# Sliding-window attention block: one V load a tile and sums turned on TensorE for the first four tiles, with a new instruction order

## The chip, the cores and the metric

The kernel runs on one core of a Trainium2 chip. The metric is device time in microseconds (us) of one execution. A core has a matrix engine (TensorE, PE in the profile), a vector engine (VectorE, DVE), an activation engine (ScalarE, ACT), a general engine (GpSimd, POOL), and a sync engine (SP) that here only issues transfers; sixteen DMA engines move the data. Each engine runs its own list of instructions in order and waits on semaphores for the others. Engines work from SBUF, the on-chip memory of 128 partitions; TensorE writes to PSUM, eight banks of 512 fp32 per partition, from which VectorE or ScalarE evict.

## The reference

One transformer block with adaptive layer norm, 2048 tokens, width 512, batch 1, bf16:

```
mod = (silu(c) @ w_mod)          # six vectors of 512: sa, ca, ga, sb, cb, gb
h = layernorm(x) * (1 + ca) + sa
q, k, v = h @ wqkv               # 32 heads of 16
# each token attends to W = 8 keys: itself and 2, 4, ... 14 tokens back (dil = 2)
idx = pos[:, None] - 2 * arange(8);  logits = (q . k[idx]) / 4, masked where idx < 0
o = softmax(logits) @ v[idx]
x = x + ga * (o @ wo)
h = layernorm(x) * (1 + cb) + sb
x = x + gb * ((silu(h @ w1) * (h @ w3)) @ w2)      # inner width 1792
```

## The kernel before

The tokens lie in 16 tiles of 128. Tile T goes through these steps; the line numbers are those of the profile.

- Layer norm statistics on VectorE (L594, L595) with the reciprocal root on GpSimd (L599, L601); the normalized tile is turned by TensorE or by a DMA transpose, and ScalarE applies the modulation (L676, L653). This is done in four groups of four tiles.
- Projections on TensorE: q and k with channels on the partitions (L777, evicted by ScalarE in L785 and L786), v with tokens on the partitions (L796). ScalarE evicts v (L806) into one of six buffers `sb_v`, with the channels put in the order (channel in head, head), and Sync stores it to a scratch tensor in HBM, `v_scratch_dram`. A V buffer is free when its store has landed.
- Logits: VectorE multiplies q by the eight shifted views of k (L827, 4096 products a partition); TensorE sums the products over each head's 16 channels with an indicator `sb_E` (L836), in four column groups of 32 tokens that run side by side. In each group the 32 tokens stand in the order even tokens first, then odd ones: the columns are read at a step of 2. For tile 0 one extra matmul (L833) adds a large negative number where a key lies before the first token; its constant is `sb_before`. Maximum, exponential (ScalarE, L866), sum and division follow for two tiles at a time (L848 to L881).
- The weights of a pair of tiles are turned by TensorE (L891) and evicted by ScalarE into `sb_al` (L895), so that a partition holds one (token pair, window place) combination.
- V load: for each quarter q of the tile one transfer of 128 pieces of 2 KB (L904): partition (t, w) gets the two neighbouring rows of V of token pair t shifted by window place w. Four loads of 256 KB a tile fill the 8 rows a partition of a `sb_vsh` buffer. There are two such buffers, and a third, `sb_vshx`, in the memory of `wqkv` once the projections are over.
- VectorE multiplies V by the weights in place (L911, 4096 elements a partition), and TensorE sums over the window places with the indicator `sb_ind` (L920). ScalarE evicts the sums to `sb_oa` (L926), a DMA transpose turns them into `sb_ot`, and TensorE projects them with `wo` (L944). VectorE adds the result to x (L948).
- The second norm (L616 to L631, GpSimd L626 and L627), and the feed-forward part in six groups of two or four tiles: gate and up on TensorE (L960), SiLU and copy on ScalarE (L966, L970), their product on VectorE (L971, L974), the down projection (L1003, L991), the last addition on VectorE (L1019) and the store of the output from one of four buffers `sb_o`.

The weights are loaded by Sync in pieces; w1 and w3 have four pieces each (`w1_0` to `w3_3`), as has w2. All of Sync's transfers share one queue.

Nothing orders this at run time. `Program.op` records every step with its engine and what it reads and writes. Two literal lists at the end of the file, `ORDER` and `SLOTS`, say in which order the recorded steps stand in the engines' lists, and which buffer each value gets; `place` applies them, `synchronize` derives the waits from them, and `emit` writes the instructions. All transfers are recorded by one helper, so that every one of them has line 124.

Of the kernel before, what the change touches and what calls it, by code (L numbers as in the profile page):

```python
# [266 lines left out]
PACKET = {T: 95 if T < 2 else 122 for T in range(16)}  # L267
WMOD = 66
WARMS = (8, 1, 1, 1, 3)
NVB = 6  # L270
# [4 lines left out]
AVCOL = frozenset(range(16))  # L275
UPACT = frozenset((g, f) for g in range(4) for f in range(14))
GBLATE = False
# [3 lines left out]
def _build(p, A_x, A_wqkv, A_wo, B_w1, B_w3, B_w2, c, w_mod, out):  # L281
# [20 lines left out]
    vshb = [sb([P, 8, D], bf, f"vsh{i}") for i in range(2)]  # L302
# [14 lines left out]
    before = sb([P, W, 2, 16], bf, "before")  # L317
# [28 lines left out]
    osb = [nc.alloc_sbuf_tensor_at(f"sb_o{i}", [P, D], bf, offset=nc.lookup_mloc(wqkv).addr + 8192 + 1024 * i) for i in range(NOB)]  # L346
    vsh_x = nc.alloc_sbuf_tensor_at("sb_vshx", [P, 8, D], bf, offset=nc.lookup_mloc(wqkv).addr)
# [31 lines left out]
    qkv_hold = held(vshpool, [vsh_x]) + held(opool, osb)  # L379

    vc, vident, vcst, vE, vind, vbefore = (Val(n) for n in ("const", "ident", "cst", "E", "ind", "before"))
# [19 lines left out]
    for edge, mult in ((0, 1), (W - 1, -1)):  # L401
# [3 lines left out]
    p.op("pool", lambda e: e.memset(before[:], 0.0), 250, k, w=[vbefore])  # L405
    p.op("pool", lambda e: e.affine_select(out=before[:], in_=before[:], compare_op=ALU.is_ge, fill=BEFORE, base=0,
                                           pattern=[[-DIL, W], [1, 2], [2, 16]], channel_multiplier=0), 400, k, w=[vbefore])
# [10 lines left out]

    def split_rows(a, row):
        return bass.AP(a.tensor, a.offset + row * D, [[D, 2], [2 * D, P // 2], [1, D]])  # L420
# [125 lines left out]
    def gate(i):  # L546
# [24 lines left out]
        p.op("act", lambda e: e.activation(dst[:], bank(vgb), ACT.Copy), c_act(512), k, r=[vgb], w=[vg[i]])  # L571
# [244 lines left out]
    def logits(Ts):  # L816

        vl = Val("ps_l", psum)
        for i, T in enumerate(Ts):
# [10 lines left out]
            def red(e, i=i, T=T, vp=vp):  # L830
                c0 = vl.at * 512 + i * W * 32
                if T == 0:
                    e.matmul(PALL[0:32, c0:c0 + W * 32], ones[:, 0:32], before[:], start=True, stop=False, tile_position=(0, 0))  # L833
                for ft in range(KT):
                    for q in range(4):
                        ins = e.matmul(PALL[32 * q:32 * q + 32, c0:c0 + W * 32], E_sb[:, ft, :], bass.AP(vp.at, ft * P + 32 * q, [[W * KT * P, P], [KT * P, W], [1, 2], [2, 16]]),  # L836
                                       start=(ft == 0 and (T > 0 or q > 0)), stop=(ft == KT - 1), tile_position=(0, 32 * q))
                return ins

            p.op("pe", red, C_RED + (110 if T == 0 else 0), ("lg", T), r=[vp, vE] + ([vbefore, vc] if T == 0 else []), part=[vl], tiled=True)  # L840
# [32 lines left out]
    def softmax(Ts, vl, ve, vx_):  # L873
# [12 lines left out]
        def turn(e):  # L886
            b = bank(vt).bitcast(bf)
            for i in range(n):
                at = b[:, i * 256:(i + 1) * 256].rearrange("p (q y h) -> p q y h", q=4, y=2)
                for y in range(2):  # L890
                    ins = e.transpose(at[:, :, y, :], bass.AP(ve.at[0], i * W * 32 + y * 16 * W, [[2 * W * 32, P], [1, P]]), ident[:])  # L891
            return ins
# [6 lines left out]
    def values(T, i, val):  # L899

        vv = Val("vsh", vshpool)
        loads = []
        for q in range(4):
            p.dma(lambda q=q: vv.at[:, 2 * q:2 * q + 2, :],  # L904
                  bass.AP(v_dram, (PAD + T * P + 32 * q) * D, [[2 * D, 16], [-DIL * D, W], [1, 2 * D]]), ("vl", T), (128, 2048),
                  r=[vv_dram[T]] + ([vv_dram[T - 1]] if T else [vvpad]), part=[vv], group=loads, cost=640, again=PACKET[T])

        def av(e):
            a_w = bass.AP(val.at, i * 8 * H, [[2 * 8 * H, P], [H, 8], [0, DH], [1, H]])
            v_w = bass.AP(vv.at, 0, [[8 * D, P], [D, 8], [H, DH], [1, H]])  # L910
            return e.tensor_tensor(v_w, v_w, a_w, ALU.mult)  # L911

        avs[T] = p.op("dve", av, C_PQ, ("av", T), r=[val], w=[vv], lock=True)
        vo, vt = Val("ps_o", psum), Val("ot", otpool)
        if T in AVCOL:
            def acc(e):
                b = bank(vo)
                for r in range(2):
# [245 lines left out]
```

## Time and profile before

| | |
|---|---|
| median of three runs | 244.95 us (243.38 to 245.19) |
| profiled execution: time, span | 245.03 us, 243.0 us |
| TensorE busy | 232.6 us, 96% of the span |
| VectorE, ScalarE, GpSimd busy | 169.1, 158.3, 23.0 us |
| moved by DMA | 38.33 MB |
| granted TensorE clock | 1.00 |

The span runs from the first to the last instruction of the profiled execution; what its time has beyond the span lies ahead of it and behind. In rows that group instructions stand line, engine, operation, what is written and read, the count, the busy time in us, the mean length of one in ns, and behind the second bar the idle time of the engine just before them, with what ended it. Rows in order of time begin with the start and the length in us. [...] In the page's second part a digit is the busy share of one fortieth of the span, in tenths.

### The profile page before, as it was taken

The numbers are of one execution on the slowest core, as the hardware profiler recorded it, in microseconds if no ns is written. First come the engines' busy times: TensorE is split into PE (matmuls) and PEld (weight loads), VectorE is DVE, ScalarE is ACT, GpSimd is POOL, SyncE is SP. The second block draws the span as 40 slices with busy tenths as digits, with TensorE's granted clock in tenths as the row PEclk, the third lists the DMA queues.
The fourth block names the chain that finished last, engine by engine and source line by source line (L and its number), as shares of the span: only waits on it lengthen the run. The fifth ranks groups of instructions, "written<-read, shape, count | busy, mean of one in ns | idle before, by whom it ended". The sixth has DMA issues, their size and how long they took to land.

```text
span 243.0 us, 4593 instructions
## 1 busy us (share of the span) xinstructions
PE 232.6 (96%) x1789; PEld 134.1 (55%) x1814; DVE 169.1 (70%) x295; ACT 158.3 (65%) x324; POOL 23.0 (9%) x54
## 2 busy tenths in 40 slices
PE   7899999999789999999999999999999999999995
PEld 1665454545357885654444444444655447576874
DVE  5489999999697999999999698366133213155242
ACT  4358597799788978777967798876653674321300
POOL 6421330011001100011000040110000100000000
DMA  5999899599589999699897824884020030011002
GB/s 167 288 361 265 272 298 215 134 272 275 175 196 291 256 242 245 154 214 137 251 227 195 237 65 68 194 182 99 3 65 1 3 86 0 0 46 43 3 23 65
DMA packets 44685, 38.33 MB, mean 158 GB/s; under 512 B 19560, under 2 KB 35960, under 8 KB 44664
## 3 DMA queue, kind: packets, MB, share of 16 engines
q1 hardware_dynamic: 44656, 38.04, 62.6%
q8 instruction: 14, 0.23, 0.4%
q14 instruction: 7, 0.06, 0.1%
q10 hardware_dynamic: 8, 0.00, 0.0%
HBM read 29.62 MB, written 4.21 MB: 139 GB/s over the span
## 4 chain that ended last, share of the span: by engine, by line
PE 65%; DMA 14%; SPq 7%; ACT 6%; DVE 5%; issue 2%; POOL 1%; ACTq 0%
PE pall L960 33%; PE pall L1003 14%; SPq L124 7%; PE pall L777 5%; DMA sb_wm_g<-in_w_mod_dram 4%; DMA sb_ot<-sb_oa 4%; PE pall L944 3%; DMA v_scratch_dram<-sb_v 3%; PE pall L991 3%; PE pall L796 2%; PE pall L920 2%; DMA sb_h<-sb_xn 2%; PE pall L836 2%; ACT sb_h L653 2%; ACT sb_xn L620 1%
## 5 line engine op out<-in xcount | busy, mean ns | idle before, releaser
L960 PE MATMUL pall<-sb_h,sb_w 128*128 128x256 bf16 (+1 forms) x668 | 103.0, 308 | 1.4 <-DMA sb_w<-in_B_w_dram 0.7
L960 PEld LDWEIGHTS pall<-sb_h,sb_w 128*128 128x128 bf16 x672 | 64.4, 98 | 38.0 <-ACT sb_hh L970 1.5
L966 ACT ACTIVATE sb_sg<-pall 128x256 bf16<-128x256 f32 (+1 forms) x84 | 35.0, 453 | 33.5 <-PE pall L960 25.9
L1003 PE MATMUL pall<-sb_w,sb_hh 128*128 128x512 bf16 x187 | 43.2, 379 | 0.6
L827 DVE TENSOR_TENSOR sb_pq<-sb_q,sb_kT 128x4096 bf16<-128x4096 bf16 x16 | 36.3, 2277 | 0.0
L970 ACT ACTIVATE sb_hh<-pall 128x256 bf16<-128x256 f32 (+1 forms) x56 | 26.5, 494 | 10.3 <-PE pall L960 10.3
L1003 PEld LDWEIGHTS pall<-sb_w,sb_hh 128*128 128x128 bf16 x196 | 18.9, 98 | 21.3 <-DVE sb_hh L971 0.6
L974 DVE TENSOR_TENSOR sb_hh<-sb_sg,pall 128x256 bf16<-128x256 bf16 x28 | 11.1, 418 | 26.6 <-PE pall L960 23.3
L911 DVE TENSOR_TENSOR sb_vsh<-sb_vsh,sb_al 128x4096 bf16<-128x4096 bf16 x12 | 27.4, 2286 | 2.4 <-ACT sb_al L895 1.3
L777 PE MATMUL pall<-sb_h,sb_wqkv 128*128 128x512 bf16 x107 | 25.8, 379 | 1.2 <-ACT sb_v L806 0.9
L971 DVE TENSOR_TENSOR sb_hh<-sb_sg,sb_hh 128x256 bf16<-128x256 bf16 (+1 forms) x56 | 17.9, 349 | 7.3 <-ACT sb_sg L966 4.0
L1019 DVE TENSOR_TENSOR sb_o<-pall,sb_x 128x512 bf16<-128x512 f32 (+1 forms) x18 | 11.0, 627 | 13.4 <-PE pall L1003 7.3
L626 POOL TENSOR_SCALAR sb_rs<-sb_var 128x2 f32<-128x2 f32 x8 | 4.9, 608 | 145.5 <-ACT sb_xn L620 145.5
L777 PEld LDWEIGHTS pall<-sb_h,sb_wqkv 128*128 128x128 bf16 x112 | 10.3, 98 | 12.0 <-ACT sb_v L806 1.4
L944 PE MATMUL pall<-sb_wo,sb_ot 128*128 128x512 bf16 x60 | 15.7, 379 | 0.9 <-DMA sb_ot<-sb_oa 0.5
L796 PE MATMUL pall<-sb_wqkv,sb_h 128*128 128x512 bf16 x61 | 15.9, 379 | 0.3 <-issue 0.2
L653 ACT ACTIVATE sb_h<-sb_h,sb_modc 128x512 bf16<-128x512 bf16 (+1 forms) x20 | 13.2, 721 | 3.9 <-DMA sb_h<-sb_xn 3.9
L948 DVE SCALAR_TENSOR_TENSOR sb_x<-pall,sb_x 128x512 bf16<-128x512 f32 x16 | 10.9, 688 | 6.5 <-PE pall L944 6.5
L631 ACT ACTIVATE sb_xn<-sb_x,sb_nb,sb_rs 128x512 bf16<-128x512 bf16 x16 | 12.6, 808 | 4.1 <-DVE sb_nb L628 4.1
L620 ACT ACTIVATE sb_xn<-sb_x,sb_nm 128x512 bf16<-128x512 bf16 x16 | 11.5, 720 | 2.9 <-DVE sb_nm L616 2.7
L785 ACT ACTIVATE sb_q<-pall 128x512 bf16<-128x512 f32 x16 | 9.3, 604 | 4.4 <-PE pall L777 4.4
L594 DVE BATCH_NORM_STATS2 sb_st<-sb_x 128x6 f32<-128x512 bf16 x15 | 9.9, 676 | 2.7 <-DMA sb_x<-in_A_x_dram 2.7
(112 smaller groups left out, 236.1 us busy)
## 6 DMA issues: line engine op xcount, KB each, us to landing
sb_vsh<-v_scratch_dram SPq DMA_DIRECT2D x48, 256.0 KB, 4.9
sb_vshx<-v_scratch_dram SPq DMA_DIRECT2D x16, 256.0 KB, 4.0
sb_w<-in_B_w_dram SPq DMA_DIRECT2D x6, 512.0 KB, 7.8
sb_w<-in_B_w_dram SPq DMA_DIRECT2D x6, 384.0 KB, 4.4
v_scratch_dram<-sb_v SPq DMA_DIRECT2D x16, 128.0 KB, 4.3
out_dram<-sb_o SPq DMA_DIRECT2D x14, 128.0 KB, 2.0
sb_x<-in_A_x_dram SPq DMA_DIRECT2D x3, 512.0 KB, 9.8
sb_wqkv<-in_A_wqkv_dram SPq DMA_DIRECT2D x2, 512.0 KB, 7.9
```

The lines of the kernel that those rows point to most:

```text
L124: return e.dma_start(a, b, transpose=True) if transpose else e.dma_start(a, b)
L653: return e.activation(vh.at[:, ft, 0:n * P], vh.at[:, ft, 0:n * P], ACT.Identity, bias=modc[:, 8 * which + ft:8 * which + ft + 1], scale=m ...
L777: ins = e.matmul(bank(vp)[:, 0:n], wqkv[:, t, kind * D + ft * P:kind * D + (ft + 1) * P], vh.at[:, t, 0:n], start=(t == ORDER[0]), stop=(t ...
L796: ins = e.matmul(bank(vp), vh.at[:, t, tt * P:(tt + 1) * P], wqkv[:, t, 2 * D:3 * D], start=(t == ORDER[0]), stop=(t == ORDER[-1]))
L827: return e.tensor_tensor(vp.at[:], in0, in1, ALU.mult)
L911: return e.tensor_tensor(v_w, v_w, a_w, ALU.mult)
L944: ins = e.matmul(bank(vy), vt.at[:, ft, :], wo[:, ft, :], start=(ft == 0), stop=(ft == KT - 1))
L960: ins = e.matmul(bank(vp)[:, 0:n], wt[:, t, fi * P:(fi + 1) * P], vh.at[:, t, 0:n], start=(t == 0), stop=(t == KT - 1))
L966: p.op("act", lambda e: e.activation(vt.at[:, 0:n], bank(vgp)[:, 0:n], ACT.Silu), c_act(n), k, r=[vgp], w=[vt], table="silu")
L970: p.op("act", lambda e: e.activation(vh_.at[:, 0:n], bank(vup)[:, 0:n], ACT.Copy), c_act(n), k, r=[vup], w=[vh_])
L971: p.op("dve", lambda e: e.tensor_tensor(vh_.at[:, 0:n], vt.at[:, 0:n], vh_.at[:, 0:n], ALU.mult), 60 + n * 69 // 128, k, r=[vt], w=[vh_], ...
L1003: ins = e.matmul(bank(vz), vhh[fi].at[:, tt * P:(tt + 1) * P], w2[:, fi, :], start=(fi == 0), stop=(fi == NF - 1))
```

## The change

For tiles 0 to 3 (the set `EARLY`):

- A partition of the V buffer now belongs to four tokens and two shifts in place of two tokens and one shift. It gets six neighbouring rows of V, 6 KB in one piece, by one transfer of 128 pieces a tile. The buffer has ten rows a partition: the rows loaded are 4 to 9, and the products of the other shift go to rows 0 to 3.
- The multiplication is done in two instructions of 2048 elements, first the one for the further shift (rows 4 to 7 into 0 to 3), then the one for the nearer shift (rows 6 to 9 in place). The indicator of the sums is `sb_ind4`, four partitions to a group.
- The order of the tokens in the logits follows: a column group q holds the tokens q, q + 4, q + 8, ... of the whole tile, so the products are read at a step of 4, and the turning of the weights reads them at a step of 2. The mask of tile 0 now concerns all four column groups: four mask matmuls instead of one, from a `sb_before` four times as large, which lies in the memory of w2; the first piece of w2 is loaded only when tile 0's sums are done.
- The column sums are turned by four TensorE transposes in place of the DMA transpose; the eviction by ScalarE from PSUM to `sb_ot` puts the tokens back in order.

For all tiles: five V buffers in place of six; two of the four output buffers lie in the memory of the two gate rows `ga_bc` and `gb_bc`, which are no longer needed then; `ORDER` and `SLOTS` are new throughout. Unused branches are removed (`GBLATE`, the other arm of `AVCOL`, `split_rows`). The diff, cut to its core:

```
-PACKET = {T: 95 if T < 2 else 122 for T in range(16)}
-NVB = 6
+NVB = 5
+WL = 4
+TB = W // WL * DIL
+NLOAD = TB + DIL
+NROW = NLOAD + TB
+EARLY = frozenset((0, 1, 2, 3))
+PACKET = {T: 264 if T in EARLY else 122 for T in range(16)}
...
-    vshb = [sb([P, 8, D], bf, f"vsh{i}") for i in range(2)]
+    vshb = [sb([P, NROW, D], bf, f"vsh{i}") for i in range(2)]
...
-    before = sb([P, W, 2, 16], bf, "before")
+    ind4 = sb([P, P // WL], bf, "ind4")
...
+    before = nc.alloc_sbuf_tensor_at("sb_before", [P, TB, W, P // WL], bf, offset=nc.lookup_mloc(w2).addr)
...
+    p.op("pool", lambda e: e.memset(ind4[:], 1.0), 100, k, w=[vind4])
+    for edge, mult in ((0, 1), (WL - 1, -1)):
+        p.op("pool", lambda e, edge=edge, mult=mult: e.affine_select(
+            out=ind4[:], in_=ind4[:], compare_op=ALU.is_ge, fill=0.0, base=edge, pattern=[[-WL * mult, P // WL]],
+            channel_multiplier=mult), 250, k, w=[vind4])
+    p.op("pool", lambda e: e.memset(before[:], 0.0), 700, k, w=[vbefore])
+    for q in range(TB):
+        p.op("pool", lambda e, q=q: e.affine_select(out=before[:, q], in_=before[:, q], compare_op=ALU.is_ge, fill=BEFORE, base=q,
+                                                    pattern=[[-DIL, W], [TB, P // WL]], channel_multiplier=0), 400, k, w=[vbefore])
...
-                if T == 0:
-                    e.matmul(PALL[0:32, c0:c0 + W * 32], ones[:, 0:32], before[:], start=True, stop=False, tile_position=(0, 0))
+                for q in range(4 if T == 0 else 0):
+                    e.matmul(PALL[32 * q:32 * q + 32, c0:c0 + W * 32], ones[:, 0:32], before[:, q], start=True, stop=False,
+                             tile_position=(0, 32 * q))
...
+                        cols = [q, [TB, 32]] if T in EARLY else [32 * q, [1, 2], [2, 16]]
...
+            if T == 0:
+                late["w2_0"].deps[o] = False
...
+                    if Ts[i] in EARLY:
+                        ins = e.transpose(b[:, (2 * i + y) * P:(2 * i + y + 1) * P],
+                                          bass.AP(ve.at[0], i * W * 32 + y, [[2 * W * 32, P], [2, P]]), ident[:])
+                        continue
...
+        if T in EARLY:
+            p.dma(lambda: vv.at[:, TB:NROW, :],
+                  bass.AP(v_dram, (PAD + T * P - DIL) * D, [[TB * D, P // WL], [-2 * DIL * D, WL], [1, NLOAD * D]]), ("vl", T),
+                  (P, 2048), r=near, w=[vv], cost=640, again=PACKET[T])
...
+            if early:
+                a_w = bass.AP(val.at, (8 * i + TB * y) * H, [[2 * 8 * H, P], [H, TB], [0, DH], [1, H]])
+                v_w = bass.AP(vv.at, (NROW - TB - DIL * y) * D, [[NROW * D, P], [D, TB], [H, DH], [1, H]])
+                o_w = bass.AP(vv.at, (NROW - TB) * (1 - y) * D, [[NROW * D, P], [D, TB], [H, DH], [1, H]])
+                return e.tensor_tensor(o_w, v_w, a_w, ALU.mult)
...
+        for y in (1, 0) if early else (0,):
+            o = p.op("dve", lambda e, y=y: av(e, y), C_PQ // 2 + 35 if early else C_PQ, ("av", T), r=[val], w=[vv], lock=True, lead=o)
...
+        if early:
+            vq = Val("ps_oT", psum)
+
+            def turn(e):
+                b = bank(vq).bitcast(bf)
+                for ft in range(KT):
+                    ins = e.transpose(b[:, ft * P:(ft + 1) * P], va.at[:, ft * P:(ft + 1) * P], ident[:])
                 return ins
+            p.op("pe", turn, 228, ("ot", T), r=[va, vident], w=[vq])
+            p.op("act", lambda e: e.activation(vt.at[:].rearrange("p k (t q) -> p k t q", q=TB),
+                                               bank(vq).bitcast(bf)[:, 0:KT * P].rearrange("p (k q t) -> p k t q", k=KT, q=TB), ACT.Copy),
+                 c_act(512), ("ot", T), r=[vq], w=[vt])
+        else:
             p.dma(lambda: vt.at[:], lambda: va.at[:], ("ac", T), (128, 1024), r=[va], w=[vt], cost=1250, transpose=True)
...
-ORDER = [...]
+ORDER = [...]
-SLOTS = [...]
+SLOTS = [...]
```

More of the change, by code (lines that the diff above doesn't have):

```diff
@@ L914, in values @@
+        avs[T] = o
         vo, vt = Val("ps_o", psum), Val("ot", otpool)
[L915 to L918, printed above, removed]
[L919 to L939 removed]
```

85 lines of the change are left out of this document (34 added, 51 removed), and 128 rows, old and new, of tables (ORDER, SLOTS).

## The prediction

> **What bounds the kernel now.** I read the page first, the windows next, and then the rows of single waits. On the page the first lines say which engine is full, and the DMA row says when the transfer engines are.
>
> ```profile
> span 243.0 us, 4593 instructions
> ...
> PE 232.6 (96%) x1789; PEld 134.1 (55%) x1814; DVE 169.1 (70%) x295; ACT 158.3 (65%) x324; POOL 23.0 (9%) x54
> ...
> DMA  5999899599589999699897824884020030011002
> ```
>
> TensorE is busy for 96% of the span, so only two things can move the time: its own work, and the some 10 us in which it stands. The DMA row is near 9 up to slice 17 (about 100 us) and low behind it. The profiled execution took 245.03 us, 2.03 more than its span, and the median of the runs is 244.95. I sum against 245.03; the difference of 0.08 is nothing here.
>
> The windows say where TensorE stands in the part that the change touches:
>
> ```profile
> core 0: us, PE busy (x) PEld busy (x) DVE busy (x) ACT busy (x) POOL busy (x), PEclk, DMA share, GB/s
> 24.00:50.00 26.00, 25.61 (x230) 13.38 (x232) 25.86 (x37) 19.43 (x37) 3.71 (x8) 1.00 0.85 222
> 50.00:62.00 12.00, 11.95 (x92) 5.86 (x91) 11.23 (x16) 9.94 (x20) 1.33 (x2) 1.00 1.05 302
> 62.00:74.00 12.00, 9.52 (x101) 5.70 (x102) 10.52 (x11) 10.76 (x24) 0.00 (x0) 1.00 0.66 176
> 74.00:103.00 29.00, 28.89 (x297) 20.90 (x298) 27.76 (x46) 24.15 (x62) 1.71 (x2) 1.00 1.01 237
> ```
>
> From 62 to 74 us TensorE loses 12.00 - 9.52 = 2.48 us; in the three other windows together 0.55. Just ahead of that hole the DMA engines are full (share 1.05 at 302 GB/s). The granted clock is 1.00 throughout and plays no part. The rows inside the hole:
>
> ```profile
> 63.06 1.04 PE L777 MATMUL pall<-sb_h,sb_wqkv 128*128 128x512 bf16 x4 [0.86 <-ACT sb_v L806]
> 64.52 0.61 PE L920 MATMUL pall<-sb_vsh,sb_ind 128*32 128x512 bf16 x8 [0.42 <-ACT sb_q L785]
> 71.77 1.49 PE L960 MATMUL pall<-sb_h,sb_w 128*128 128x256 bf16 x12 [0.75 <-DMA sb_w<-in_B_w_dram]
> 73.84 1.04 PE L944 MATMUL pall<-sb_wo,sb_ot 128*128 128x512 bf16 x4 [0.36 <-DMA sb_ot<-sb_oa]
> ...
> 62.20 2.29 DVE L911 TENSOR_TENSOR sb_vsh<-sb_vsh,sb_al 128x4096 bf16<-128x4096 bf16 x1 [0.91 <-DMA sb_vsh<-v_scratch_dram]
> ...
> ACT sb_v L806 <- DMA v_scratch_dram<-sb_v: 2.1, 1, 2.1
> ...
> 54.39 7.94 DMA v_scratch_dram<-sb_v
> ```
>
> The last row is of the chain of waits: a V store issued at 54.39 landed 7.94 us later, behind all that stood in the rings. The eviction of the next V tile (L806) needs that store's buffer and waited 2.1 us, TensorE waited for it (0.86 and 0.42), and the last gate or up weights (0.75), tile 3's V load (0.91 on VectorE) and tile 3's DMA transpose (0.36) were late too. The idle of the four TensorE rows is 2.39 us. A row's idle counts from the modelled end of the matmul before. A 512-column matmul lasts 379 ns in the record, and four together last 1.04, which is (1.04 - 0.38) / 3 = 0.22 apart; so each stop costs up to 0.16 more than the row says. The hole is worth 2.4 to 3.0 us, and every row of it leads to a transfer.
>
> **The change, part by part.**
>
> *V loads.* Tiles 0 to 3 had four loads of 256 KB each; they get one of 128 x 6 KB = 768 KB. Four tiles move 16 x 256 - 4 x 768 KB = 1.05 MB less.
>
> ```profile
> sb_vsh<-v_scratch_dram SPq DMA_DIRECT2D x48, 256.0 KB, 4.9
> ...
> L124 SPq DMA_TRANSPOSE sb_ot<-sb_oa x16: 1189/1212/2098, 44.2 to 176.5; - x16
> ...
> DMA to landing us min/median/max: 2.3/3.5/6.6
> ...
> 68.27 5.52 DMA sb_ot<-sb_oa
> ...
> 50.03 1.83 SPq L124 DMA_DIRECT2D sb_vsh<-v_scratch_dram  x3
> ```
>
> At the 302 GB/s of the full window that is 3.5 us of all DMA engines, at the 222 of the window before it 4.7. If a 6 KB piece moved at half the rate of a 2 KB one, the load would last 1.5 times the old four and the four tiles would cost more, by about 7 us of DMA; no row has such a piece. I take 4 us saved, since bytes and not counts fill the rate in all four windows. Sync's queue loses 12 issues of 0.61 and four transposes of 1.21, some 12 us, of which the chain holds none: Sync waits elsewhere.
>
> *DMA transposes of tiles 0 to 3.* They go; in their place stand four 128-column transposes on TensorE and one ScalarE eviction a tile.
>
> ```profile
> 31.22 0.83 PE L668 MATMUL pall<-sb_ident,sb_xn 128*128 128x128 bf16 x12
> ...
> L668 PE MATMUL pall<-sb_ident,sb_xn 128*128 128x128 bf16 x48 | 4.6, 219 | 0.1
> ...
> L926 ACT ACTIVATE sb_oa<-pall 128x512 bf16<-128x512 f32 x16 | 9.5, 600 | 2.5 <-PE pall L920 2.4
> ...
> L806 ACT ACTIVATE sb_v<-pall 128x512 bf16<-128x512 f32 x16 | 9.6, 606 | 2.9 <-DMA v_scratch_dram<-sb_v 2.1 <-PE pall L796 0.8
> ```
>
> One transpose lasts 219 ns, but twelve take 0.83, so they stand (0.83 - 0.22) / 11 = 0.055 apart: 16 of them are **+0.9 us** of TensorE, all on the path. Each waits for L926's 0.60; in the new order TensorE has 0.86 to 1.8 us of projection matmuls between the column sums and the transposes, so that wait is covered, and costs up to 0.6 a tile if they are late. The eviction reads PSUM with a stride; so does L806, at 606 ns against 600 for the plain L926. Four are 2.4 us of ScalarE, which has 26.00 - 19.43 and 12.00 - 9.94 free there. Behind tile 0's eviction ScalarE holds a gate copy, the exponential of tiles 2 and 3 and a K eviction; VectorE waits for the second, TensorE for the third. They come at most one transposing group, 0.4 us, later, and I take nothing. The way from the column sums to the output projection becomes 0.2 + 0.6 us and two handovers instead of a landing (3.5 us in the median, 5.52 for tile 3's, which ended in the stop at 73.84), so the 0.36 goes.
>
> [...]
>
> *VectorE.* One multiplication of 4096 elements becomes two of 2048, with the two tiles' halves interleaved.
>
> ```profile
> L911 DVE TENSOR_TENSOR sb_vsh<-sb_vsh,sb_al 128x4096 bf16<-128x4096 bf16 x12 | 27.4, 2286 | 2.4 <-ACT sb_al L895 1.3 <-DMA sb_vsh<-v_scratch_dram 1.2
> L1046 DVE TENSOR_TENSOR sb_w<-sb_w,sb_gb_bc 128x2048 bf16<-128x2048 bf16 x2 | 2.4, 1219 | 0.0
> ```
>
> 2 x 1.22 - 2.29 = +0.15 a tile, +0.6 in all, on an engine that is 99% busy from 24 to 50 us. It is hidden only by the distance between a product and its matmul; without that cover it costs 0.6. I take 0.
>
> *Logits and weights order.* The sums read the products at a step of 4 elements instead of 2, and the attention transposes at 2 instead of 1.
>
> ```profile
> L836 PE MATMUL pall<-sb_pq,sb_E 128*32 128x256 bf16 x256 | 8.9, 271 | 0.0
> ```
>
> At a step of 2, 256 such matmuls take 8.9 us, four side by side. Step 4 is shown nowhere: between nothing and twice the time for 64 of them, +2.2. I take 0, since step 2 shows no loss. Three more mask matmuls in tile 0 are under +0.1.
>
> *GpSimd.* The mask is four times as large, and the 4-wide indicator is new.
>
> ```profile
> 8.00 0.54 POOL L406 TENSOR_SCALAR_AFFINE_SELECT sb_before<-sb_before 128x256 bf16<-128x256 bf16 x1
> ...
> 9.38 0.31 POOL L396 TENSOR_SCALAR_AFFINE_SELECT sb_E<-sb_E 128x128 bf16<-128x128 bf16 x1
> 16.12 0.22 POOL L599 TENSOR_SCALAR sb_rs<-sb_mv 128x2 f32<-128x2 f32 x1 [6.43 <-DVE sb_mv L595]
> ```
>
> Three selects of 0.54, two small ones and longer memsets are 3 to 4 us in front of the next L599, which has 6.43 us of idle ahead of it: 0. The mask now lies in w2's memory, so the first w2 load waits for tile 0's logits; in the new order it stands behind the loads of tile 5, long after them: 0.
>
> *The order.* Everything is placed anew. I count the columns in the two programs' lists of TensorE instructions at the spacing above (0.216 for 512, the rest in proportion). The first gate matmul moves from 56.8 to 58.6 us of TensorE work while tile 1's projection, its source, moves from 43.4 to 42.2: 3 us more slack. The same count between the last projection of tiles 4 to 7 and the first gate matmul of their group goes from 11.7 to 14.9. There the old order stops:
>
> ```profile
> 111.05 4.70 DMA sb_h<-sb_xn x2
> ...
> 118.99 1.34 PE L960 MATMUL pall<-sb_h,sb_w 128*128 128x512 bf16 x5 [0.49 <-ACT sb_h L653]
> ```
>
> I take that stop as gone, 0.5 as the row has it (0.8 by the spacing). Against it: fewer V buffers (5 for 6), see the second rival.
>
> **Sum.** 245.03 - 3.0 (hole) - 0.8 (stop at 118.99) + 0.9 (transposes) + 0.1 (mask) = **242.2**. With the smaller readings, 2.4 and 0.5, and VectorE's 0.6 paid it is 243.7.
>
> **The rivals.**
>
> *The old stops stay.* DMA stays full to 103 us (1.01) and other loads fill the gap; then only the added work counts: 245.03 + 1.0 = 246.0, or 245.2 with the stop at 118.99 gone; 245.6 between them. For it: from 24 to 103 us the DMA engines do 0.85 x 26 + 1.05 x 12 + 0.66 x 12 + 1.01 x 29 = 72 us of work, of which 4 is little. Against it: the hole is short and the 7.94 us of backlog is what makes it. This is also the case in which the wide load brings nothing.
>
> *V buffers run out (slower).* In the new order Sync issues the loads of tiles 2 and 3 only when tile 0's and 1's sums are done, and behind these stand the V stores of tiles 6, 4, 7 and 8, each with 0.8 to 2.1 MB of loads ahead of it: 3 to 8 us at the 222 / 0.85 = 261 GB/s of the window from 24 to 50. With five buffers an eviction waits for the store five tiles back; if that store lands later than the matmuls come, ScalarE stands, and with it TensorE. Once it cost 0.86 + 0.42 and the drains, 1.6 us; four times is 6.4: 242.2 + 6.4 = 248.6. It decides where a store's landing takes more than about 6 us from its issue.
>
> *Other stops close too.*
>
> ```profile
> 103.00:118.00 15.00, 14.81 (x121) 8.23 (x125) 14.31 (x23) 11.74 (x25) 1.86 (x4) 1.00 1.06 183
> 119.00:152.00 33.00, 32.50 (x206) 14.95 (x210) 28.73 (x43) 26.48 (x48) 3.10 (x3) 1.00 0.69 163
> ```
>
> TensorE stands for 0.19 and 0.50 us here and for 0.55 in the windows from 24 to 103 outside the hole: 1.24, or near 2 with a drain at each stop. A new order without any: 242.2 - 1.6 = 240.6. Against it: no change of this kind has a reason to close stops that it doesn't touch.
>
> *Slow TensorE reads.* Step 4 at half rate gives 242.2 + 2.2 = 244.4; transposes that each last their full 219 ns give 242.2 + 3.5 - 0.9 = 244.8.
>
> **How the numbers follow.** Forecast 242.2 (its own range 240.8 to 243.7): 0.44. Other stops close too, 240.6: 0.15. Old stops stay, 245.6: 0.16. Slow TensorE reads, 244.4 to 244.8: 0.06. V buffers, 248.6: 0.19. A change of 1% is 2.45 us, about what a measurement can tell: faster means under 242.5. Some six tenths of the forecast and all of the other-stops case lie there: 0.28 + 0.15 = 0.43. Slower means over 247.4: 0.19. The rest, 0.38, is within 1%. The range from 239.5 to 247.5 leaves out the V-buffer case and nothing else; its low end is the other-stops case with the full 2 us and a little of the hole's drains on top.
>
> **What would show it.** Right: from about 60 to 75 us TensorE has no wait for L806's successor nor for gate or up weights; the V stores land in under 6 us; the sixteen new transposes stand 0.05 to 0.06 apart; logits matmuls keep 271 ns and four side by side; DVE halves take 1.2. Wrong: a new wait of TensorE for ScalarE behind V evictions, DMA full with the same backlog, or a hole that has moved to another place in the new order, which no count of columns excludes.

## The result and the profile after

The changed kernel takes 242.83 us in the median (242.04 to 244.05, 19 runs), the kernel before 244.97 (242.79 to 245.48, 19 runs) beside it: a ratio of 0.9931, 95% interval 0.9914 to 0.9947. That is a gain of 0.7%: clear of no change at all, but inside the 1% within which the prediction counts a kernel as neither faster nor slower. The forecast was 242.2. The profiled execution took 243.03 us with a span of 241.3, against 245.03 and 243.0 before.

The page of the changed kernel, with two of the rows that the prediction read on the page of before:

```profile
span 241.3 us, 4649 instructions
...
PE 235.5 (98%) x1833; PEld 136.5 (57%) x1833; DVE 170.0 (70%) x299; ACT 159.1 (66%) x328; POOL 24.8 (10%) x60
```

TensorE is busy for 2.9 us more in a span that is 1.7 us shorter. The windows of the changed kernel, with the limits of the prediction (the fifth reaches to 119, to take in the stop at 118.99, and the last is new):

```profile
24.00:50.00 26.00, 26.00 (x218) 12.88 (x216) 24.22 (x31) 19.12 (x36) 3.91 (x4) 1.00 0.77 228
50.00:62.00 12.00, 12.00 (x134) 6.42 (x132) 11.03 (x17) 11.63 (x24) 1.34 (x3) 1.00 0.91 306
62.00:74.00 12.00, 12.00 (x109) 7.22 (x106) 11.93 (x17) 11.64 (x26) 0.93 (x2) 1.00 0.95 259
74.00:103.00 29.00, 29.00 (x283) 21.77 (x281) 28.87 (x45) 25.03 (x65) 0.41 (x1) 1.00 0.68 169
103.00:119.00 16.00, 16.00 (x154) 8.81 (x152) 15.66 (x27) 13.08 (x24) 1.67 (x4) 1.00 0.91 181
119.00:152.00 33.00, 33.00 (x211) 15.13 (x209) 27.54 (x40) 25.65 (x48) 1.85 (x4) 1.00 0.66 171
152.00:238.00 86.00, 86.00 (x551) 52.18 (x550) 32.53 (x73) 40.26 (x87) 2.39 (x4) 1.00 0.15 44
```

The number behind the window's length is TensorE's busy time, and it equals the length in each: TensorE does not stand from 24 to 238 us. The view of waits, cut to TensorE, has three rows, all in the first 15 us:

```profile
PE pall L549 <- DVE sb_ones L390: 1.5, 1, 1.5
PE pall L741 <- DMA sb_wqkv<-in_A_wqkv_dram: 1.0, 1, 1.0
PE pall L515 <- DMA sb_wm_s<-in_w_mod_dram: 0.5, 1, 0.5
```

From the prediction's rows of before, the idle in these windows up to 152 us adds up to 0.39 + 0.05 + 2.48 + 0.11 + 0.19 + 0.50 = 3.72, with the stop at 118.99 (0.49) 4.21 us. All of it is gone, and so is another 0.37 between 152 and 238 us. The groups by form say what came in its place:

```profile
L848 PE MATMUL pall<-sb_pq,sb_E 128*32 128x256 bf16 x256 | 10.6, 305 | 0.0
L816 ACT ACTIVATE sb_v<-pall 128x512 bf16<-128x512 f32 x16 | 9.7, 614 | 1.4 <-PE pall L806 1.4
L939 DVE TENSOR_TENSOR sb_vsh<-sb_vsh,sb_al 128x2048 bf16<-128x2048 bf16 x8 | 9.3, 1216 | 0.2 <-ACT sb_al L914 0.2
L970 ACT ACTIVATE sb_ot<-pall 128x512 bf16<-128x512 bf16 x4 | 2.3, 600 | 0.1
L966 PE MATMUL pall<-sb_ident,sb_oa 128*128 128x128 bf16 x16 | 1.4, 219 | 0.0
```

L848 is the line that was L836: the same 256 logits matmuls now cover 10.6 us in place of 8.9. That is 1.7 us which the prediction took as 0. L816 was L806, the V eviction: it waits for no store any more. The sixteen transposes (L966) and the two halves of the multiplication (L939) are of the forecast size. The balance in this trace: 4.2 + 0.4 of stops gone and 2.9 of busy time added make -1.7, as the spans differ. Of the 2.9 the logits are 1.7 and the transposes 0.9; the other 0.3 no single row shows.

The logits of single tiles in order of time show where the 1.7 lies. "Groups" are here the four matmuls that run side by side, one in each column group. First tile 1 of the kernel before, then tiles 1 and 0 of the changed one, with tile 0's mask ahead of its sums:

```profile
26.86 0.63 PE L836 MATMUL pall<-sb_pq,sb_E 128*32 128x256 bf16 x16
```

```profile
28.52 1.08 PE L848 MATMUL pall<-sb_pq,sb_E 128*32 128x256 bf16 x16
29.41 0.30 PE L843 MATMUL pall<-sb_before,sb_ones 128*32 128x256 bf16 x4
29.54 1.08 PE L848 MATMUL pall<-sb_pq,sb_E 128*32 128x256 bf16 x16
```

Sixteen sums are four such groups. Before, the groups stand (0.63 - 0.27) / 3 = 0.12 apart; in the changed tiles (1.08 - 0.42) / 3 = 0.22. From tile 4 on, at a step of 2, nothing has changed. Four tiles of four groups, each 0.11 longer, make 1.76. (A distance is worked out from a row: its length less that of one matmul, divided by the number of matmuls or groups behind the first. Records overlap in all sizes here: a single one of 512 columns lasts 379 ns and they stand 0.22 us apart, one of 256 in these sums at a step of 2 271 ns and 0.11 to 0.12, one of 128 219 ns and 0.055.)

### The profile page after: what moved, and what is told of

It is laid out like the page before. It is cut to its first block, busy times and chain, and to the rows that moved or that the text cites. A ratio compares the mean times of both kernels' runs of the same rounds, so it can differ in the third digit from the quotient of the medians.

```text
span 241.3 us, 4649 instructions
## 1 busy us (share of the span) xinstructions
PE 235.5 (98%) x1833; PEld 136.5 (57%) x1833; DVE 170.0 (70%) x299; ACT 159.1 (66%) x328; POOL 24.8 (10%) x60
## 2 busy tenths in 40 slices
DMA packets 40782, 36.76 MB, mean 152 GB/s; under 512 B 17192, under 2 KB 33592, under 8 KB 40760
## 3 DMA queue, kind: packets, MB, share of 16 engines
q1 hardware_dynamic: 40752, 36.47, 55.6%
HBM read 28.57 MB, written 4.21 MB: 136 GB/s over the span
## 4 chain that ended last, share of the span: by engine, by line
PE 92%; DMA 3%; ACT 2%; SPq 2%; issue 0%; DVE 0%
PE pall L995 41%; PE pall L1038 18%; PE pall L787 10%; PE pall L979 6%; PE pall L806 4%; PE pall L848 4%; PE pall L953 3%; DMA sb_wm_s<-in_w_mod_dram 3%; PE pall L1026 3%; SPq L124 2%; ACT sb_h L686 1%; PE pall L751 1%; ACT sb_q L795 1%; PE pall L678 1%; PE pall L910 1%; ACT sb_kT L761 0%
## 5 line engine op out<-in xcount | busy, mean ns | idle before, releaser
L1001 ACT ACTIVATE sb_sg<-pall 128x256 bf16<-128x256 f32 (+1 forms) x84 | 36.9, 462 | 41.6 <-PE pall L995 39.4
L1038 PE MATMUL pall<-sb_w,sb_hh 128*128 128x512 bf16 x196 | 45.4, 379 | 0.0
L787 PE MATMUL pall<-sb_h,sb_wqkv 128*128 128x512 bf16 x112 | 27.4, 379 | 0.1
L942 DVE TENSOR_TENSOR sb_vsh<-sb_vsh,sb_al 128x4096 bf16<-128x4096 bf16 x9 | 20.5, 2282 | 0.0
L636 POOL TENSOR_SCALAR sb_rs<-sb_var 128x2 f32<-128x2 f32 x8 | 2.5, 313 | 148.9 <-ACT sb_xn L630 148.9
L806 PE MATMUL pall<-sb_wqkv,sb_h 128*128 128x512 bf16 x64 | 16.4, 379 | 0.0
```

What stands on the lines that cost most here:

```text
L787: ins = e.matmul(bank(vp)[:, 0:n], wqkv[:, t, kind * D + ft * P:kind * D + (ft + 1) * P], vh.at[:, t, 0:n], start=(t == ORDER[0]), stop=(t ...
L806: ins = e.matmul(bank(vp), vh.at[:, t, tt * P:(tt + 1) * P], wqkv[:, t, 2 * D:3 * D], start=(t == ORDER[0]), stop=(t == ORDER[-1]))
L1001: p.op("act", lambda e: e.activation(vt.at[:, 0:n], bank(vgp)[:, 0:n], ACT.Silu), c_act(n), k, r=[vgp], w=[vt], table="silu")
L1038: ins = e.matmul(bank(vz), vhh[fi].at[:, tt * P:(tt + 1) * P], w2[:, fi, :], start=(fi == 0), stop=(fi == NF - 1))
```

## The experiments

Two things were open. The forecast number was nearly met, but with one large term at zero and other stops closed too, so the reasons had to be tested apart: was it the relief of the DMA rings that closed the hole, and was it the step of 4 that made the logits slow.

### Is it the traffic? The bytes put back

```
+            p.dma(lambda: vv.at[:, 0:2, :],
+                  bass.AP(v_dram, (PAD + T * P) * D, [[2 * D, 16], [-DIL * D, W], [1, 2 * D]]), ("vl", T), (128, 2048), r=near, part=[vv])
```

> The changed kernel with the traffic of the old loads put back: each of the first four tiles also loads 256 KB of V rows into the free part of its buffer, which nobody reads, 1.05 MB in all, and the multiplication waits for it as for the wide load. Theory (the relief of the DMA rings closed the hole): the hole comes back, 2 to 3 us, 244.8 to 245.8. Rival (the new order closed it, since the loads now stand far enough ahead of their use): no more than 0.3 us, 242.8 to 243.1.

Measured: 242.88 us, ratio to before 0.9926 (0.9899 to 0.9954). Two of its windows:

```profile
50.00:62.00 12.00, 12.00 (x134) 6.45 (x133) 11.03 (x16) 11.63 (x23) 1.34 (x3) 1.00 1.07 335
62.00:74.00 12.00, 12.00 (x110) 7.36 (x109) 11.93 (x18) 11.62 (x27) 0.92 (x2) 1.00 0.95 261
```

The DMA engines are at least as full as in the kernel before (1.07 and 0.95 against 1.05 and 0.66), and TensorE still does not stand. In the new order the megabyte is worth nothing: by the ratios 0.1 us less than the changed kernel, with an interval of some 0.7 us, and by the trace no stop at all. The relief theory falls for this order, as far as the V rows go. The run does not put back all of the relief: the four DMA transposes moved another 0.52 MB, and the packets of the large queue take 56.8% of the span here, against 62.6% before and 55.6% in the changed kernel. With all of the old traffic the new order ran only in the run with the old operations, below.

### Is it the traffic? The bytes taken from the old kernel

```
-        for q in range(4):
+        for q in range(2 if T in (2, 3) else 4):
```

> The kernel before, in its own order, with two of the four 256 KB loads of V left out for tiles 2 and 3 (the multiplication then takes rows that an earlier tile left there, so the values of these two tiles are not the reference's): 1.05 MB less, just ahead of the hole. Theory (the backlog in the DMA rings makes the hole, as the rows of its waits say): the hole closes and the rest stays, 245.0 - 2.5 = 242.5. Rival (when the transfers come earlier, ScalarE is late next, as in the run of the changed operations in the old order): a part of it, 243.5 to 244.5. Rival (the order alone): 245.0.

Measured: 243.65 us, ratio 0.9959 (0.9933 to 0.9985). The window of the hole in its profiled execution, and then TensorE's two longest waits behind the first 24 us:

```profile
62.00:74.00 12.00, 11.59 (x123) 8.01 (x123) 10.88 (x17) 10.75 (x25) 0.00 (x0) 1.00 0.69 174
```

```profile
PE pall L960 <- ACT sb_h L653: 0.4, 1, 0.4
PE pall L960 <- DMA sb_w<-in_B_w_dram: 0.4, 1, 0.4
```

In the old order the relief does work: the idle of the hole falls from 2.48 to 0.41 us, and no eviction of V waits for a store. By the ratio it is 1.0 us (0.4 to 1.6), less than the 2.5 by which the span of the one profile is shorter; that execution is the fastest of the ten. Part of the idle comes back behind the hole: 0.55 us from 74 to 103 us, where it was 0.11. The number is that of the second outcome. Its reason, that ScalarE is late next, the trace does not show: what is left lies in several small waits, and the longest for ScalarE (0.4, `sb_h`) was there before.

### The new operations in the old order

The edit is in `ORDER` and `SLOTS`: operations that both kernels have stand where they stood. The sixth V buffer lies in the first Q tile's memory:

```
+    v_hold = held(vpool, [nc.alloc_sbuf_tensor_at("sb_v5", [P, D], bf, offset=nc.lookup_mloc(qb[0]).addr)])
```

> The changed kernel's operations in the order of the kernel before: each operation that both have stands where it stood, the wide load where the first of the four loads stood, the transposes on TensorE and their eviction where the DMA transpose was issued; a sixth V buffer lies in the memory of the first Q tile once that is free, since the old order needs six, and the buffers are dealt out anew. Theory (the operations relieve the DMA rings and that closes the hole, whatever the order): the hole at 62 to 74 us goes, the stop near 119 us stays: 245.0 - 2.5 + 0.9 (transposes) + 1.8 (step-4 reads) = 245.2. Rival (the order closed the stops): the hole stays, 245.0 + 2.7 = 247.7.

Measured: 247.0 us, ratio 1.0084 (1.0055 to 1.0112): slower than before. The window of the hole, and then TensorE's two longest waits behind the first 24 us:

```profile
62.00:74.00 12.00, 10.60 (x111) 6.37 (x110) 11.31 (x11) 11.26 (x22) 0.00 (x0) 1.00 0.47 122
```

```profile
PE pall L980 <- ACT sb_ot L971: 1.4, 1, 1.4
PE pall L807 <- ACT sb_h L664: 0.8, 1, 0.8
```

No row of its waits leads to a V store or to gate and up weights, and the DMA share of the window is 0.47 where it was 0.66. But ScalarE is late instead: the projection waits 1.4 us for the new eviction (L971 here, L970 in the changed kernel), which stands behind a table load of 1.28 us and the gate's activations in ScalarE's order. So the operations remove the stops that the prediction traced to transfers and add 2.7 us of TensorE work and a stop on ScalarE. Neither theory's number was met; the rival's, 247.7, is nearer, for another reason than it gave. The stop near 119 us, which was expected to stay, is gone too: from 103 to 152 us TensorE stands for 0.11 in all.

### The old operations in the new order

Only `ORDER` and `SLOTS` change, on the kernel before.

> The reverse of the run in the old order: the operations of the kernel before (four V loads, DMA transposes, one product a tile, step 2) in the order of the changed kernel, each where its counterpart stands, the DMA transpose right behind the eviction of the sums; buffers dealt out anew, six V buffers. From the column sums of tiles 0 to 3 to their projection the new order has 3.3, 4.6, 5.3 and 3.6 us of TensorE work, and eviction and DMA transpose need 0.6 + 3.3 or more behind 0.45 of sums. Theory (the order closes the stops of the old program, but is possible only with the transposes on TensorE): no stop for V stores, weights or loads, but new ones at the projections of tiles 0 to 3, 1 to 2 us each at two or more of them: 245.0 - 4.2 + 2 to 6 = 243 to 247. Rival (the order is enough by itself): 241 to 242. Rival (the operations closed the hole): the stops for V stores and weights are there too, over 247.

Measured: 250.66 us, ratio 1.0253 (1.0209 to 1.0297). Two rows of TensorE's waits, then three windows of 4 us, then rows of TensorE in order of time inside them:

```profile
PE pall L944 <- DMA sb_ot<-sb_oa: 3.8, 3, 1.8
PE pall L521 <- DMA sb_wm_s<-in_w_mod_dram: 2.1, 1, 2.1
```

```profile
50.00:54.00 4.00, 1.91 (x26) 0.97 (x25) 3.65 (x6) 3.31 (x9) 0.00 (x0) 1.00 0.95 360
54.00:58.00 4.00, 3.93 (x33) 1.99 (x31) 0.51 (x3) 0.64 (x3) 0.93 (x2) 0.62 1.06 279
58.00:62.00 4.00, 4.00 (x21) 1.84 (x20) 2.38 (x2) 3.21 (x6) 0.00 (x0) 0.96 1.07 279
```

```profile
53.53 0.17 PE L521 MATMUL pall<-sb_mbase,sb_ident 128*128 128x8 bf16 x1 [2.09 <-DMA sb_wm_s<-in_w_mod_dram]
53.56 0.95 PE L524 MATMUL pall<-sb_csz,sb_wm_s 128*128 128x8 bf16 x32
...
55.50 1.91 PE L796 MATMUL pall<-sb_wqkv,sb_h 128*128 128x512 bf16 x4
```

The time is over 247, as the third outcome had it, but the mechanism is that of the first: stops at the projections (L944) for the DMA transposes, 3.8 us in three. With all of the old traffic no eviction of V waits for a store and no matmul for gate and up weights. Above the expected 243 to 247 it comes by a stop of 2.1 us for modulation weights, which was not expected, and by what follows it: the clock column falls to 0.62 from 54 to 58 us, and four 512-column matmuls take 1.91 there in place of 1.03. The weights are late by the DMA transposes as well, as Sync's rows show:

```profile
45.02 2.50 SPq L124 DMA_TRANSPOSE sb_ot<-sb_oa  x2
47.57 0.58 SPq L124 DMA_DIRECT2D sb_wm_s<-in_w_mod_dram  x1
```

Two transposes, which wait for their `sb_oa`, stand ahead of this load in Sync's list; in the changed kernel they are not there, and the load is issued at 42.19.

These four runs together: the new operations in the old order lose, the old operations in the new order lose, and both together gain. The new order puts the projections of tiles 0 to 3 some 3.3 to 5.3 us of TensorE work behind their column sums, which the turning on TensorE can meet and a DMA transpose cannot. That the order leaves room for the V stores and for gate and up weights is shown by the bytes put back and by the old operations in the new order; in the latter other stops lie ahead, which leave transfers more time. Which of its many moves does it was not tried singly.

### The step of the logits reads

Q and K of the first four tiles are evicted in another order of tokens, so that the sums read at a step of 2 and get the same tokens; VectorE then needs three products a tile. The core:

```
-                        cols = [q, [TB, 32]] if T in EARLY else [32 * q, [1, 2], [2, 16]]
+                        cols = [64 * (q // 2) + q % 2, [2, 32]] if T in EARLY else [32 * q, [1, 2], [2, 16]]
...
+                dst = bass.AP(k0, ft * 2 * KB + 8, [[KT * 2 * KB, P], [KB, 2], [2, 128], [1, 2]])
```

> The changed kernel, but the Q and K of the first four tiles are evicted in another order of tokens (pairs of tokens of every second pair first), so that the logits sums of tiles 0 to 3 read at a step of 2 elements again in place of 4. Everything else, the order too, is as in the changed kernel; VectorE gets three products in place of one for each of the four tiles, and GpSimd one small copy; K of the first four tiles lies in w2's memory. Theory (the step-4 read runs at half rate and is paid in full, because TensorE is never idle from 24 to 238 us): the 16 groups of four sums stand 0.107 us apart in place of 0.216, 16 x 0.11 = 1.8 us less, so 242.8 - 1.8 = 241.0, ratio to the kernel before 0.984. Rival (something else, such as VectorE with its two more instructions a tile, some 0.15 x 2 x 4 = 1.2 us, sets the time there): the groups get closer but TensorE waits for sb_pq or sb_al instead, 242.5 to 244. Rival (the distance is not due to the step): groups stay at 0.216 and the time at 242.8.

Measured: 241.3 us, ratio 0.987 (0.9821 to 0.9919). The groups by form of this kernel (L878 is the logits line, L855 and L858 the products of tiles 0 to 3, L864 those of the others):

```profile
L864 DVE TENSOR_TENSOR sb_pq<-sb_q,sb_kT 128x4096 bf16<-128x4096 bf16 x12 | 27.3, 2284 | 0.0
...
L878 PE MATMUL pall<-sb_pq,sb_E 128*32 128x256 bf16 x256 | 8.8, 272 | 0.0
L858 DVE TENSOR_TENSOR sb_pq<-sb_q,sb_k 128x1024 bf16<-128x1024 bf16 x8 | 5.2, 686 | 0.0
L855 DVE TENSOR_TENSOR sb_pq<-sb_q,sb_k 128x2048 bf16<-128x2048 bf16 x4 | 4.8, 1212 | 0.0
```

The logits are back at 8.8 us, and the kernel gets 1.5 faster. The products cost (4.8 + 5.2) / 4 - 2.28 = 0.22 us more of VectorE a tile, and from 24 to 50 us VectorE is then busy for 25.98 of 26 us, while TensorE idles for 0.13 again, as the window of this kernel shows:

```profile
24.00:50.00 26.00, 25.87 (x224) 12.96 (x223) 25.98 (x42) 20.66 (x38) 3.34 (x6) 1.00 0.78 242
```

So the step-4 read is the cause, and paid nearly in full. To set this version beside the changed kernel, both ran again on one chip:

> The kernel of the first run of this study again (step 2 reads through another order of Q and K in tiles 0 to 3), beside the changed kernel on the same chip. By the first run 241.3 against 242.8: 0.985 to 0.990 of the kernel before, and 1.5 us below the changed kernel. If the first run was a chance, both come out at 242.8.

> The changed kernel itself, beside the run above on the same chip: 242.8, 0.993 of the kernel before.

Measured: 241.6 us, ratio 0.9878 (0.9831 to 0.9926), against 242.95, ratio 0.9914 (0.9882 to 0.9946). The medians are 1.35 apart here and 1.5 by the first run. The intervals of the ratios still overlap, but four of this version's six runs here lie below all nine of the changed kernel, and the logits row changes to match. Its medians are below those of both kernels.

### Which reads are slow

The logits of the four tiles are read in four ways.

```
+STEPS = ([[32 * q, [1, 32]] for q in range(4)], [[64 * (q // 2) + q % 2, [2, 32]] for q in range(4)],
+         [[2 * q, [8, 16], [1, 2]] for q in range(4)], [[q, [3, 32]] for q in range(4)])
```

> The changed kernel, with the logits sums of tile 0 read contiguously, of tile 1 at a step of 2 elements, of tile 2 in pairs of neighbours 8 elements apart, of tile 3 at a step of 3; the tokens are then not those of the reference in these tiles. [...] Rival (what counts is the distance of one column from the next): pairs at 0.107 to 0.16. The time is 242.8 less 1.76 x the share of groups that get fast.

Measured: 241.07 us in a single execution. Rows in order of time: tile 1 (step 2), tile 0 (contiguous), tile 2 (pairs of neighbours 8 apart):

```profile
27.66 0.65 PE L850 MATMUL pall<-sb_pq,sb_E 128*32 128x256 bf16 x16
...
28.25 0.60 PE L850 MATMUL pall<-sb_pq,sb_E 128*32 128x256 bf16 x16
```

```profile
41.83 1.09 PE L850 MATMUL pall<-sb_pq,sb_E 128*32 128x256 bf16 x16
```

The groups stand 0.12, 0.11 and (1.09 - 0.41) / 3 = 0.23 us apart; in the trace tile 3's, at a step of 3, start at 42.715, 42.907, 43.082 and 43.255, 0.18 apart. Pairs of neighbours are as slow as step 4, although half of their columns lie side by side: the rival, which had them at 0.107 to 0.16, falls. By the stretch of elements over which the 32 tokens of a window place are spread, the rows are in order: at 32 (contiguous) and 64 (step 2) the groups stand 0.11 to 0.12 apart, at 96 (step 3) 0.18, at 128 0.23 (pairs) and 0.22 (the changed kernel's step of 4). Why the reads over more than 64 take longer no run shows. The single execution lies 0.7 below what these distances make of 242.8 (1.0 less); that stays open.

Whether one stream alone is slow (A), or only four together (B):

```
+EXTRA = {0: [(0, 0, 4)] * 8, 1: [(0, 0, 2)] * 8, 2: [(0, 0, 4), (1, 1, 4)] * 4, 3: [(0, 0, 4), (1, 0, 4), (2, 0, 4), (3, 0, 4)] * 4}
+                for q, off, step in EXTRA.get(T, ()):
+                    e.matmul(PALL[32 * q:32 * q + 32, c0:c0 + W * 32], E_sb[:, 0, :],
+                             bass.AP(vp.at, off, [[W * KT * P, P], [KT * P, W], [step, 32]]),
+                             start=True, stop=True, tile_position=(0, 32 * q))
```

> The changed kernel with extra sums ahead of those of tiles 0 to 3, overwritten by the real ones: in tile 0 eight at a step of 4 that follow one another in one quarter of the columns, alone; in tile 1 the same at a step of 2; in tile 2 four pairs side by side at step 4; in tile 3 four groups of four side by side at step 4 that all read the same elements. Theory A (each stream by itself is slow at step 4): alone 0.21 us apart, pairs and fours too. [...] The time is 242.8 plus 1.7 to 2.6 for B or 3.4 to 5 for A.

Measured: 248.15 us in a single execution. The rows in order of time show the extra sums (L844) of tile 1 and of tile 0, six each before other matmuls mix in:

```profile
29.10 0.84 PE L844 MATMUL pall<-sb_pq,sb_E 128*32 128x256 bf16 x6
...
30.90 1.54 PE L844 MATMUL pall<-sb_pq,sb_E 128*32 128x256 bf16 x6
```

Alone, step 2 stands (0.84 - 0.27) / 5 = 0.11 apart and step 4 (1.54 - 0.41) / 5 = 0.23. So A: a stream at a step of 4 is slow by itself, and B falls. The extra sums of tiles 2 and 3 stand 0.23 apart as well, but they did not run as planned: the quarters (the four column groups) did not start together. Tile 3's on the same elements ran two at a time beside two real sums on others, in all rounds but one. So two streams on equal elements are no faster, and for four the trace has only that one round, which also took 0.23. At these distances the extra sums come to at most 8 x 0.11 + 16 x 0.23 = 4.6 us, 247.4; the last 0.8 of the single execution stays open.

### The transposes, doubled

```
-                for ft in range(KT):
+                for ft in list(range(KT)) * 2:
```

> The changed kernel with each of the sixteen new TensorE transposes of the attention outputs done twice; the output is the same. Theory (they are pipelined and on the path): 16 x 0.055 = 0.9 us more, 243.7. [...] Rival (hidden): 242.8.

Measured: 243.51 us, ratio 0.995 (0.992 to 0.998). The transposes in its groups by form:

```profile
L966 PE MATMUL pall<-sb_ident,sb_oa 128*128 128x128 bf16 x32 | 2.3, 219 | 0.0
```

The busy time grows from 1.4 to 2.3 us, 0.9 for sixteen more, and the median by 0.7 against 242.83. That agrees with 0.055 each. The intervals of the two ratios overlap, so the time alone would not tell 0.9 from 0; the busy time does, with TensorE idle for 0.00 us from 24 to 238. The 0.219 of a single record is its length and not its price in a row. The 3.5 us more that sixteen times this length would make are excluded.

### One V buffer fewer

```
-NVB = 5
+NVB = 4
```

> The changed kernel with four V buffers in place of five; five V stores stand up to 56 places earlier in the list, as four buffers need, and buffers are dealt out anew. Theory (with five no eviction of V waited for a store, and there is slack to spare): 242.8 to 243.3. Rival (the V buffers are next to bind, the slower case of the prediction with its mechanism one buffer on): evictions of V wait for stores and TensorE for them, 244.4 to 249.

Measured: 251.96 us, ratio 1.0311 (1.0263 to 1.0359). The waits of all engines that begin the matter, and TensorE in steps of 4 us:

```profile
ACT sb_v L816 <- DMA v_scratch_dram<-sb_v: 6.2, 3, 2.7
...
DVE sb_vsh L939 <- DMA sb_vsh<-v_scratch_dram: 4.3, 2, 2.2
...
PE pall L953 <- DVE sb_vsh L939: 4.1, 1, 4.1
```

```profile
62.00:66.00 4.00, 0.25 (x8) 0.14 (x12) 2.66 (x3) 1.34 (x3) 0.00 (x0) 1.00 1.08 378
66.00:70.00 4.00, 3.78 (x38) 1.49 (x32) 4.00 (x4) 1.99 (x4) 0.00 (x0) 0.57 1.10 336
70.00:74.00 4.00, 4.00 (x32) 1.99 (x34) 3.21 (x5) 2.88 (x7) 0.00 (x0) 1.00 0.93 280
```

The slower rival's mechanism, one buffer further on, at more than its price: evictions of V wait 6.2 us for stores, the late multiplication stops TensorE for 4.1 us, and the clock is granted at 0.57 for the next four. Five buffers show no such wait (L816 above), but they have no whole buffer to spare. Five stores stand up to 56 places earlier in this list than in the changed kernel, as four buffers need, so the run is not the buffer count alone.

### One piece or three

```
+            for j in range(3):
+                p.dma(lambda j=j: vv.at[:, TB + 2 * j:TB + 2 * j + 2, :],
+                      bass.AP(v_dram, (PAD + T * P - DIL + 2 * j) * D, [[TB * D, P // WL], [-2 * DIL * D, WL], [1, 2 * D]]), ("vl", T),
+                      (P, 2048), r=near, part=[vv], group=loads, cost=640, again=PACKET[T])
```

> The changed kernel with each wide load of six rows a partition (6 KB a packet) as three loads of two rows (2 KB): the same bytes and order, eight more DMA issues in all. Theory (bytes and not packets set the rate of the rings, as the prediction took it): landings of about 6.6 us, the same packet time in sum, 242.8. Rival (2 KB packets take longer for their bytes: 121 ns against 274 ns for 6 KB in the trace of the changed kernel): 4 x (3 x 121 - 274) x 384 packets over 16 engines, near 2 us a tile of more DMA time, and still 242.8, since nothing waits for it.

Measured: 243.62 us in a single execution. The row of the page for the large DMA queue (packets, MB, share of the engines' span), first of this kernel, then of the changed one:

```profile
q1 hardware_dynamic: 41904, 36.47, 55.6%
```

```profile
q1 hardware_dynamic: 40752, 36.47, 55.6%
```

1152 more packets for the same bytes, and the same share of the DMA engines' time. For these loads the bytes and not the packets set the DMA time, as the prediction took it; the difference of packet lengths that the rival pointed at does not appear in the sum. (From its figures it would be 89 ns x 128 packets over 16 engines, 0.7 us a tile and not 2, or 1.2% of the span for the four tiles.) The landing of a whole load cannot be read here, since the pieces land one by one.

## Why the prediction was right, and where not

**The number** came out 0.6 from the forecast, and that is in part luck. 242.2 was made of two stops gone, 2.48 + 0.49 = 2.97 us of idle (3.8 with the allowance for drains), and 1.0 of work added. In the trace 4.6 of idle are gone and 2.9 of work is added: 1.6 more of the one and 1.9 more of the other, two errors that nearly cancel. The allowance is the rest of what the span shows otherwise than forecast, 1.7 less in place of 2.8; the median came out 2.1 less.

**The hole** closed, with 2.48 of idle, as forecast. The reason given, that every row of it leads to a transfer, so that lighter rings close it, holds in part for the old order (1.0 us of the 2.4 to 3.0, by the run with half the loads) and not for the new one (0.0 by the bytes put back). The step that failed is the inference from "the rows lead to transfers" to "less traffic is the cure": how far the order sets the use behind the transfer mattered more. The landings of the V stores say the same, from the view of `sb_v`, first before, then after:

```profile
DMA to landing us min/median/max: 1.9/4.3/7.9
```

```profile
DMA to landing us min/median/max: 1.7/4.5/7.5
```

They were to be under 6 us if the mechanism was right. They are as slow as they were; nobody waits for them.

**The relief** was taken as 1.05 MB and 4 us of the DMA engines. It left out what the four DMA transposes moved: the whole goes from 38.33 to 36.76 MB, 1.57 less, and the packets of the large queue from 62.6% of 243.0 us to 55.6% of 241.3, 18 us less. The term was sized too small, but the sum did not depend on it: it took the whole hole as gone.

**The stop at 118.99** is gone, as forecast from the columns counted between source and use. The count is not shown to be the reason: with the new operations in the old order the stop is gone too, while with half the loads in the old order a wait of 0.4 for the same value stays.

**The transposes** cost 0.9 on the path, spaced as predicted. The new eviction (600 ns) is hidden in the new order; in the old one TensorE waited 1.4 for it once.

**Logits at a step of 4**: taken as 0 "since step 2 shows no loss", with 2.2 as the other end. It was 1.7. This is the term that was mis-sized. Step 2 was no evidence: contiguous reads and step 2 stand the same 0.11 to 0.12 us apart, step 3 0.18 and step 4 0.22 to 0.23, and no logits row of before had a step over 2.

**VectorE**, +0.15 a tile (2 x 1.216 against 2.28), and **GpSimd**, with no wait behind it, cost nothing, as taken.

**The rivals.** The other stops closed too: 0.39 + 0.05 + 0.11 + 0.19 + 0.50 = 1.24 us of idle is gone. The argument against it, that the change has no reason to close stops that it doesn't touch, overlooked that a wholly new order is itself such a reason. Slow reads came true by their first mechanism. Both happened together with the forecast hole, a mixture that the prediction priced only one by one. The V buffers do not bind at five, though stores land up to 7.5 us after their issue: "more than about 6 us" was not the point from which it decides. How far behind the store the eviction stands in the order must count as well; that distance was not varied by itself. The case in which the old stops stay did not happen.

## What to carry to other kernels

Where the busiest engine is at 96%, count what an edit adds to that engine as closely as what it relieves: here slower reads took back 1.7 of the 4.6 us of stops, and another order of tokens in two kinds of evictions removed that. An access pattern that no row of the profile shows is worth a small run of its own before it is taken as free. And an operation and the order it stands in are one change: each alone made this kernel slower.

## What the runs showed of the hardware that was not expected

Logits matmuls of 256 columns, four side by side, follow each other at 0.11 to 0.12 us at a step of 1 or 2 bf16 elements, 0.18 at 3 and 0.22 to 0.23 at 4, and as much in neighbouring pairs 8 apart. One stream alone is no faster: 0.11 at a step of 2, 0.23 at 4.

Two stops of TensorE cost more than themselves. In the run with four V buffers 4.1 us without work are followed by 4 us at a granted clock of 0.57; in the old operations' run in the new order 2.1 us without work and 0.95 us of 8-column matmuls are followed by 4 us at 0.62. By the clock column that is (1 - 0.57) x 4 = 1.7 us of TensorE's work lost in the first, and 0.38 x 4 + 0.04 x 4 = 1.7 in the second. In windows of 2 us the column shows 0.62, 0.53 and then 1.00 in the first, from 66 us on, and 0.73, 0.50, 0.91 and 1.00 in the second, from 54 us on. Behind shorter stops it stayed at 1.00: one of 1.8 us in the second of these runs (for `sb_ot`, between 62 and 74 us), one of 1.4 us in the run of the new operations in the old order, and the stops of the kernel before, none over 1.0 us behind the first 24. How long a stop has to be before the clock falls, and whether the 8-column matmuls had a part in the second fall, these traces do not show.
